# FNet mixing and an ELU layer: the first folds of x in another order, two column sums put off, and the middle token's second layer moved behind the last product

## The chip, the cores and the metric

One core of a Trainium2 chip runs the kernel. The metric is the device time in microseconds (us). Five engines work side by side, each through its own instructions in the order in which the program gives them: TensorE (PE in the profile, its weight loads PEld), VectorE (DVE), ScalarE (ACT), GpSimd (POOL) and SyncE (SP, which here issues DMAs). They wait for one another through semaphores.

## The reference

```python
X = np.fft.fft(x, axis=1)          # x: (8, 3008, 256)
X = np.fft.fft(X, axis=2)
x = X.real.reshape(8 * 3008, 256)
h = x @ w_in                       # w_in: (256, 2048)
g = np.where(h > 0.0, h, 1.0 * (np.exp(np.minimum(h, 0.0)) - 1.0))
return g @ w_out                   # w_out: (2048, 256)
```

All is float32 in value. The kernel receives the two weight matrices as 64-bit words and converts them itself.

## The kernel before

**The transform over the sequence** uses symmetry. A batch of x is loaded as four tiles `xl0` to `xl3` (in the code `L[0]` to `L[3]`), two by SP (first `L[3]`, then `L[0]`) and two by indirect DMAs of POOL (first `L[2]`, then `L[1]`). `fold_x` (L498) names its steps by keys. `e0` to `e3` add mirrored channels of a tile, `o0` to `o3` subtract them (one instruction of 128x768 each), `c0` to `c3` copy six columns that stand alone (128x6). `E0` adds e0 and e1, `E2` adds e2 and e3, `EO0` adds E0 and E2, `EO1` subtracts them; `O0`, `O2`, `EO2` and `EO3` do the same with the o tiles. For the first batch all of this is VectorE's work; `x1` (a row copied from `L[0]` to `L[1]`) and a one-element write that holds back `load_mats(1, 0)` are ScalarE's. `fold_first` (L549) makes four tiny sums of channel 128 of all four tiles.

A `Dft` (L607) is one product with a matrix of cosines or sines, in an even and an odd half (`mms`, six matmuls each on TensorE): `x_even` (channel 128, from `fold_first`), `R_even` (from EO0), `I_even` (from EO2), `R_odd` and `I_odd`. `copy` (ScalarE) and `unfold` (VectorE, two instructions) make the even half's columns. `plus` writes the lower 377 columns of the first 752 of a ring tile, `minus` the upper ones, one VectorE instruction each, both from the two halves (`R_even.minus` writes one column more). The rings are `Rr`, `Ir` and `Rb`; ScalarE copies Rb's rows 96 to 127 to `Ir` before `I_even` writes `Ir`.

**The two layers** run over tiles of 256 columns of the rings; a step is one tile with 256 of the 2048 hidden units. A step's first layer is `mm_P` (ring Rr, `bank("H")`), `even_part` (VectorE; reads Rb, `wex` and H, writes `E`), `mm_Q` (ring Ir), `h_minus`. Its ELU follows on ScalarE and VectorE, its second layer on TensorE. Two tiles are interleaved for the first 16 slots, so that slots 0 and 1 need the first chunk of `w_in`, slots 2 and 3 the second, and so on.

**The weights** come in 16 chunks. A chunk is converted by `fields` (two VectorE instructions, L256 and L262), `power` (for all but the first: three of ScalarE), `round` (GpSimd), `scale` (VectorE L310, then a GpSimd product, and for chunks of `w_in` two GpSimd sums, `pair`, written to `raw`). The first chunk is converted by VectorE alone except for one ScalarE instruction; its `scale` is L310 and L319. `fold_chunk(c)` (L427) multiplies a `w_in` chunk by the channel transform on TensorE; `put_chunk` (ScalarE) writes it to `Ws` and `Wc`. `turn_last_row` (TensorE) and `put_last_row` (ScalarE) make `wex`.

**Order.** Work is entered as events `at(t, fn)` (L1128); at the end they are sorted by t and run one after another. `pin` keeps each engine's instructions in that order. T is 4.8; negative times are the start. The events that are not part of the change and matter here: `dft_now(x_even)` at -13.1 and -13.08, `dft_now(R_even)` at -13.0 and -12.9, `turn_last_row(0)` at -10.6, `put_last_row(0)` at -10.59, `dft_now(I_even, 0)` at -10.5, `I_even.copy` at -1.8, `mm_P` of slot 0 at 0.0, `dft_now(I_even, 1)` at 0.05, `mm_P` of slot 1 at 0.1, `even_part` of slot 0 at 0.4, `I_even.unfold` at 0.5, `even_part` of slot 1 at 0.7, `fields` of the first `w_out` chunk at 0.96, EO1 at 1.3, `mm_Q` of slot 0 at 2.17, `fold_chunk(1)` at 2.3, `mm_Q` of slot 1 at 2.6, `dft_now(R_odd, 0)` at 3.1.

**The middle token** of every batch (position 1504) stands outside the rings. `mid_mm` (L1050) makes its hidden values for all eight batches, `mid_below`, `exp_neg` and `mid_g` its ELU, `mid_out` (L1067) its second layer (16 products, 32 matmul records), `mid_copy` takes the sums out, `mid_pick` (one product, two records) adds four row groups, `mid_store` takes them out and stores them by SP. There are 376 steps (`total`); `last` is 336.

**The end.** The last tile is combined and turned by VectorE in pieces (`comb_half`, `turn_half`); its stores are issued by SP and ACT in turn.

Of the kernel before, what the change touches and what calls it, by code (L numbers as in the profile page):

```python
# [18 lines left out]
ND = 256  # L19
# [3 lines left out]
RUN = HALF // 2  # L23
TW = 256
RING = 8 * TW
NE = 377
# [80 lines left out]
def kernel(  # L107
# [7 lines left out]
    nc = tc.nc  # L115
    NB = x.shape[0]
# [18 lines left out]
    pin = tc.keep_in_program_order  # L135
# [189 lines left out]
    def w1_dst(c):  # L325
        q, half = divmod(c, 2)
        if q not in w1:
            t = spool.tile([128, 1024], FP, tag="ot", bufs=2, name="w1")
            w1[q] = t.rearrange("p (h n) -> p h n", h=2)
        return w1[q][:, :, half * 256 : (half + 1) * 256]  # L330
# [17 lines left out]
    w1_chunks = [  # L348
        Chunk(
            moe_w_in[:, c * 256 : (c + 1) * 256].rearrange("(h p) n -> p h n", p=128),  # L350
            lambda c=c: w1_dst(c),
            IN_HOMES[c],
            IN_TMP[c],
            c > 0,
            c > 0,
        )
# [21 lines left out]
    def load_mats(ri, kodd, cuts=()):  # L378
        n = (2 * ri + kodd) * BW
        ends = (0, *cuts, BW)  # L380
        for a, z in zip(ends, ends[1:]):
            nc.sync.dma_start(
                out=MC[ri, kodd][:, a:z], in_=MC_dr.ap()[:, n + a : n + z]
            )
# [4 lines left out]
    Ir = cpool.tile([128, RING], FP, tag="Ir")  # L389
    Rb = cpool.tile([128, RING], FP, tag="Rb")  # L390
# [30 lines left out]
    def act(o, i, func=AF.Copy, **kw):  # L421
        pin(nc.scalar.activation(out=o, in_=i, func=func, **kw))  # L422
# [75 lines left out]
    def fold_x(L, engine_of, pieces):  # L498

        ops = {}  # L500

        def op(key, o, a, b, f):
            tt = lambda o, a, b, f: pin(
                engine_of(key).tensor_tensor(out=o, in0=a, in1=b, op=f)  # L504
            )
            n = o.shape[1]
            cuts = [n * i // pieces for i in range(pieces + 1)]
            for i in range(pieces):
                c = slice(cuts[i], cuts[i + 1])
                ops[key, i] = lambda c=c: tt(o[:, c], a[:, c], b[:, c], f)  # L510

        E, O = [], []
        for j in range(4):
            e = spool.tile([128, 6 * 128], FP, tag=f"e{j}", bufs=1, name=f"e{j}")
            o = spool.tile([128, 6 * 128], FP, tag=f"o{j}", bufs=1, name=f"o{j}")
            ev, ov = (
                t.rearrange("p (m o d) -> p m o d", o=2, d=64) for t in (e, o)
            )
            src = L[j].rearrange("p (m d) -> p m d", d=ND)
            if j in (1, 2):  # L520
                src = src[:, ::-1]

            lo, hi = (
                t.rearrange("p m (d o) -> p m o d", o=2)
                for t in (src[:, :, 1:129], src[:, :, 255:127:-1])
            )
            op(f"e{j}", ev, lo[:, :, ::-1], hi[:, :, ::-1], ALU.add)
            ops[f"c{j}", 0] = lambda e=ev[:, :, 0, 63:64], s=src[:, :, 0:1]: pin(
                engine_of("c").tensor_copy(out=e, in_=s)
            )  # L530
            op(f"o{j}", ov, lo, hi, ALU.subtract)
            E.append(e)
            O.append(o)
        ops["x1", 0] = lambda: act(L[1][0:1, 5 * ND :], L[0][0:1, 0:ND])
        op("E0", E[0], E[0], E[1], ALU.add)
        op("E2", E[2], E[2], E[3], ALU.add)
        op("EO0", E[1], E[0], E[2], ALU.add)
        op("EO1", E[3], E[0], E[2], ALU.subtract)
        op("O0", O[0], O[0], O[1], ALU.subtract)
        op("O2", O[2], O[2], O[3], ALU.subtract)  # L540
        op("EO2", O[1], O[0], O[2], ALU.subtract)
        op("EO3", O[3], O[0], O[2], ALU.add)
        return [E[1], E[3], O[1], O[3]], ops
# [5 lines left out]
    def fold_first(L):  # L549

        c = [t.rearrange("p (m d) -> p m d", d=ND)[:, :, 128:129] for t in L]
        c[1], c[2] = c[1][:, ::-1], c[2][:, ::-1]
        a = spool.tile([128, 6], FP, tag="xa", bufs=1, name="xa")
        g = spool.tile([128, 6], FP, tag="xg", bufs=1, name="xg")
        vtt(a.unsqueeze(2), c[0], c[1], ALU.add)
        vtt(g.unsqueeze(2), c[2], c[3], ALU.add)
        d = state["x_odd"] = spool.tile([128, 6], FP, tag="xd", bufs=1, name="xd")
        vtt(d, a, g, ALU.subtract)
        e = spool.tile([128, 6], FP, tag="xe0", bufs=1, name="xe0")
        vtt(e, a, g, ALU.add)  # L560
        return e
# [267 lines left out]
    def exp_neg(ap):  # L829
        act(ap, ap, func=AF.Exp, scale=-1.0)  # L830
# [247 lines left out]
            )  # L1078

    def mid_copy():  # L1080
        act(state["mh"][:, 0:ND], state["mo"][:, 0:ND])

    def mid_pick():
        po = state["mo"] = bank("H")
# [1 line left out]

    def mid_store():
        ob = state["mr"][0:NB, 0:ND]
        act(ob, state["mo"][0:NB, 0:ND])
        nc.sync.dma_start(  # L1090
            out=bass.AP(
                tensor=out.tensor,
                offset=out.offset + HALF * ND,
                ap=[[SEQ * ND, NB], [1, ND]],
            ),
            in_=ob,
        )

    state = {}
# [7 lines left out]
    for load in loads:  # L1107
        load()
    load_mats(0, 0, (BE,))
    w1_chunks[1].load()  # L1110
    nc.sync.dma_start(out=pick, in_=PK_dr.ap())
    EO, ops = fold_x(
        L_first, lambda key: nc.vector, 1
    )

    def fold_now(keys):
        for key in keys.split():
            ops[key, 0]()

    def dft_now(d, par, tag):  # L1120
        d.mms(par, bank(tag))

    R_even, I_even = Dft(0, 0, 0, EO[0]), Dft(1, 0, 0, EO[2])
# [4 lines left out]
    def at(t, fn):  # L1128
        events.append((t, len(events), fn))
# [16 lines left out]
    def begin_x_even():  # L1146
        state["x_even"] = Dft(0, 0, 0, fold_first(L_first), ring=Rb, first=True)

    at(-25.5, load_rest)
    at(-25.0, lambda: fold_now("e3 c3"))  # L1150
    at(-24.9, w1_chunks[0].scale)
    at(-24.8, lambda: fold_now("o3 e2 c2 E2 o2 O2"))
    at(-24.5, begin_x_even)
    at(-24.4, lambda: fold_now("e0 c0 e1 c1 E0 EO0"))
    at(-20.7, lambda: load_mats(1, 1))
    at(-20.6, w1_chunks[5].load)
    at(-20.5, w2_chunks[5].load)
# [4 lines left out]
    at(-13.08, lambda: dft_now(state["x_even"], 1, "pD"))  # L1162
    at(-13.0, lambda: dft_now(R_even, 0, "pA"))
    at(-12.9, lambda: dft_now(R_even, 1, "pB"))
    at(-11.1, lambda: state["x_even"].unfold())
    at(-11.0, lambda: fold_now("o0 o1 O0 EO2"))
    at(-10.95, R_even.copy)
    at(-10.94, R_even.unfold)
    at(-10.9, R_even.plus)
    at(-10.89, R_even.minus)  # L1170
    at(-10.85, lambda: state["x_even"].plus())
    at(-10.84, lambda: state["x_even"].minus())
    at(-10.83, lambda: act(Ir[96:128, 0:RUN], Rb[96:128, 0:RUN]))
    at(-10.92, w1_chunks[1].fields)
    at(-10.91, w1_chunks[1].power)
    at(-10.5, lambda: dft_now(I_even, 0, "pC"))
    at(-10.88, w1_chunks[1].round)
    at(0.05, lambda: dft_now(I_even, 1, "M"))
    at(-10.82, w1_chunks[1].scale)
    at(1.3, lambda: fold_now("EO1"))  # L1180

    T = PERIOD
    for chunk, k in (
# [22 lines left out]
        dt = first[k] if k < 4 else (-0.5, 0.05, 0.06, 2.95)  # L1206
# [24 lines left out]
    total = n_tiles * 8  # L1231
# [105 lines left out]
    def begin_folds(b):  # L1337
        state["EO"], state["ops"] = fold_x(state["L"], lambda key: nc.gpsimd, 2)

    steps_b = HALF * 8 // TW  # L1340
    for t, fn in (
        (-1.8, I_even.copy),
        (0.5, I_even.unfold),
        (0.6, I_even.plus),
        (0.8, I_even.minus),
        (3.1, lambda: dft_now(R_odd, 0, "pA")),
        (3.2, lambda: dft_now(R_odd, 1, "pB")),
        (T + 2.6, R_odd.copy),
        (T + 4.15, R_odd.unfold),
        (T + 4.2, R_odd.plus),  # L1350
        (T + 4.21, R_odd.minus),
    ):
        at(t, fn)
# [8 lines left out]
    for n in range(16):  # L1362
        j, k = divmod(n, 4)
# [17 lines left out]
    for b in range(1, NB):  # L1381
# [15 lines left out]
        n = 0  # L1397
# [16 lines left out]
    last = total - 40  # L1414
# [1 line left out]
        (last - 8) * T,  # L1416
        lambda: nc.sync.dma_start(out=Rx4[127:128, 0:NB], in_=r4_dr),
    )
    for n, (dt, fn) in enumerate(
        (  # L1420
            (4.75, mid_mm),
            (1.46, mid_below),
            (1.6, lambda: exp_neg(state["mr"])),
            (1.0, mid_g),
            (4.76, mid_out),
            (1.46, mid_copy),
            (4.75, mid_pick),
            (1.46, mid_store),
        )
    ):  # L1430
        at((last + n) * T + dt, fn)
    for _, _, fn in sorted(events, key=lambda e: e[:2]):
        fn()

# [29 lines left out]
```

## Time and profile before

| | |
|---|---|
| runs before (7) | median 1954.28 us, 1952.29 to 1955.21 |
| the profiled execution | 1954.53 us |
| its span, first to last instruction | 1952.5 us |
| busy: PE, PEld, DVE, ACT, POOL | 99%, 85%, 67%, 44%, 71% |
| granted TensorE clock, mean | 0.999 |

In the page's slices of the span (forty of 48.8 us each) PE is at nine tenths or more in all but the first and the last. A line of the timeline gives the start in us, the time taken, the engine, the line of the code (often a helper's, as L410 for all matmuls), the operation, the tile written and the tiles read, and in brackets how long the engine was idle just before and what ended that. A line of the table by stage gives, for each engine, the busy us and in brackets the number of instructions, then the granted clock of TensorE (PEclk), the busy share of the DMA engines and GB/s.

### The profile page before, as it was taken

The page shows a single profiled execution, that of the slowest core. Times are in us where ns is not written, and L with a number is a line of the kernel's source. Part 1 is how long each engine was busy: PE and PEld are TensorE (multiplying, and loading weights), DVE is VectorE, ACT ScalarE, POOL GpSimd, SP SyncE. Part 2 cuts the span into 40 slices and gives each one's busy share as a digit, 9 for nine tenths or more (in the row PEclk, how much of TensorE's full clock was granted, in tenths as well). Part 3 has the DMA queues.
Part 4 walks back from the last instruction along what each step waited for, and adds up shares of the span by engine and source line. Part 5 has one row for each costly group of instructions (what it writes and reads, how often), then busy time and mean ns, then how long its engine had stood idle before and what let it go on. Part 6 is the DMA issues. An engine that isn't in the chain of part 4 may idle for free.

```text
span 1952.5 us, 26991 instructions
## 1 busy us (share of the span) xinstructions
PE 1935.6 (99%) x8912; PEld 1652.9 (85%) x8912; DVE 1300.1 (67%) x2397; ACT 865.1 (44%) x1669; POOL 1379.3 (71%) x1816
## 2 busy tenths in 40 slices
PE   8999999999999999999999999999999999999998
PEld 5788788888888888888888888888888888888887
DVE  8976666666667666666666666676666666666666
ACT  3654444444444444444344444444434444444443
POOL 3888767776678766777677876777767776555655
PEclk9999999999999999999999999999999999999999
DMA  8246120101101021010210202012020110100101
GB/s 310 66 30 51 28 55 20 47 15 26 42 20 44 15 44 28 18 47 13 53 24 13 50 9 58 12 20 59 7 52 12 20 22 15 17 12 12 23 9 24
DMA packets 263290, 70.25 MB, mean 36 GB/s; under 512 B 248606, under 2 KB 249522, under 8 KB 263152
## 3 DMA queue, kind: packets, MB, share of 16 engines
q1 hardware_dynamic: 257360, 55.69, 15.0%
q0 software_dynamic: 3616, 12.59, 2.0%
q8 instruction: 70, 1.15, 0.2%
q14 instruction: 68, 0.56, 0.1%
q10 hardware_dynamic: 2176, 0.26, 0.1%
HBM read 43.66 MB, written 24.80 MB: 35 GB/s over the span
## 4 chain that ended last, share of the span: by engine, by line
PE 93%; DVE 3%; POOL 2%; issue 1%; ACT 1%; DMA 1%; SPq 0%; DVEq 0%; POOLq 0%
PE H L410 37%; PE pC L410 16%; PE pD L410 16%; PE pB L410 16%; PE pA L410 8%; POOL WT L419 1%; POOL w L419 1%; POOL G L419 0%; DMA xl<-in_x_dram 0%; DVE E L809 0%; DVE e L504 0%; DVE G L835 0%; DVE o L504 0%; DVE pow L310 0%; DMA xl<-in_x_dram,ix 0%
## 5 line engine op out<-in xcount | busy, mean ns | idle before, releaser
L419 POOL TENSOR_TENSOR G<-G 128x256 f32<-128x256 f32 x1440 | 1037.0, 730 | 511.2 <-DVE G L835 342.2
L809 DVE SCALAR_TENSOR_TENSOR E<-Rb,wex,H 128x256 f32<-128x256 f32 x752 | 327.8, 477 | 543.9 <-PE H L410 540.4
L422 ACT ACTIVATE G<-H 128x512 f32<-128x512 f32 x376 | 224.6, 597 | 959.0 <-DVE G L819 958.9
L410 PE MATMUL H<-Ir,Ws 128*128 128x256 f32 x1504 | 387.0, 380 | 3.7 <-DVE E L809 2.6
L410 PE MATMUL H<-Rr,Wc 128*128 128x256 f32 x1504 | 387.1, 380 | 0.1
L410 PE MATMUL pC<-G,WT 128*128 128x256 f32 x1440 | 369.5, 379 | 0.0
L410 PEld LDWEIGHTS H<-Rr,Wc 128*128 128x128 f32 x1504 | 284.5, 190 | 56.5 <-issue 3.4
L410 PEld LDWEIGHTS H<-Ir,Ws 128*128 128x128 f32 x1504 | 278.5, 189 | 52.0 <-DVE E L809 5.6
L410 PEld LDWEIGHTS pC<-G,WT 128*128 128x128 f32 x1440 | 273.6, 190 | 37.2
L819 DVE SCALAR_TENSOR_TENSOR G<-E,H 128x512 f32<-128x512 f32 x376 | 257.0, 684 | 41.7 <-POOL G L419 6.0
L835 DVE SCALAR_TENSOR_TENSOR G<-G,H 128x512 f32<-128x512 f32 x376 | 256.1, 681 | 42.7 <-ACT G L422 42.7
L835 DVE SCALAR_TENSOR_TENSOR G<-M,G 128x512 f32<-128x512 f32 x376 | 257.1, 684 | 0.0
L422 ACT ACTIVATE G<-G 128x512 f32<-128x512 f32 x376 | 233.2, 620 | 0.0
L410 PE MATMUL pD<-G,w 128*128 128x256 f32 x784 | 229.4, 379 | 0.5 <-POOL G L419 0.5
L410 PE MATMUL pA<-G,w 128*128 128x256 f32 x784 | 229.3, 379 | 0.6 <-DVE bs L416 0.6
L410 PE MATMUL pB<-G,w 128*128 128x256 f32 x784 | 229.3, 379 | 0.0
L422 ACT ACTIVATE M<-G 128x512 f32<-128x512 f32 x376 | 223.9, 596 | 0.0
L422 ACT ACTIVATE M<-M 128x512 f32<-128x512 f32 x376 | 221.0, 588 | 0.0
L410 PE MATMUL pB<-G,WT 128*128 128x256 f32 x720 | 214.8, 380 | 0.4
L410 PE MATMUL pD<-G,WT 128*128 128x256 f32 x720 | 214.1, 379 | 0.0
L410 PEld LDWEIGHTS pD<-G,w 128*128 128x128 f32 x784 | 148.9, 190 | 21.1 <-POOL G L419 0.9
L410 PEld LDWEIGHTS pA<-G,w 128*128 128x128 f32 x784 | 148.9, 190 | 21.1 <-issue 0.9
(145 smaller groups left out, 1416.7 us busy)
## 6 DMA issues: line engine op xcount, KB each, us to landing
out_dram<-ot SPq DMA_DIRECT2D x496, 32.0 KB
xl<-in_x_dram SPq DMA_DIRECT2D x16, 512.0 KB
xl<-in_x_dram SPq DMA_DIRECT2D x16, 256.0 KB
out_dram<-ot SPq DMA_DIRECT2D x256, 2.0 KB
Rb<-r SPq DMA_DIRECT2D x10, 376.0 KB
raw<-in_moe_w_in_dram SPq DMA_DIRECT2D x7, 512.0 KB
MC<-dft_mats SPq DMA_DIRECT2D x3, 943.5 KB
raw<-in_moe_w_out_dram SPq DMA_DIRECT2D x4, 512.0 KB
```

The lines of the kernel that those rows point to most:

```text
L410: nc.tensor.matmul(out_, lhsT=lhsT, rhs=rhs, start=start, stop=stop, skip_group_check=True)
L419: pin(nc.gpsimd.tensor_tensor(out=o, in0=a, in1=b, op=op))
L422: pin(nc.scalar.activation(out=o, in_=i, func=func, **kw))
L809: nc.vector.scalar_tensor_tensor(out=S.E[:, c], in0=Rb[:, cols(i)], scalar=wex[:, f : f + 1], in1=S.H[:, c], op0=ALU.mult, op1=ALU.add,)
L819: nc.vector.scalar_tensor_tensor(out=two(S.G[:, 0:512])[:, :, ::-1], in0=two(S.E), scalar=2.0, in1=two(S.H), op0=ALU.mult, op1=ALU.subtract,)
L835: nc.vector.scalar_tensor_tensor(out=o, in0=e, scalar=-1.0, in1=h, op0=ALU.add, op1=ALU.max)
```

## The change

- `c0`, `c2` and `c3` of the first batch go from VectorE to ScalarE; `c1` stays.
- `scale` of the first chunk moves ahead of `load_rest` and all folds.
- The folds on VectorE were e3 c3, [scale], o3 e2 c2 E2 o2 O2, [fold_first], e0 c0 e1 c1 E0 EO0, [x_even.unfold], o0 o1 O0 EO2. They become [scale], e3 c3 e0 c0 e2 c2 E2, [fold_first], e1 c1 E0 EO0, o3 o2 O2, [x_even.unfold], o0 o1 O0 EO2.
- After the unfolds, VectorE's order was fields of chunk 1, R_even.plus and minus, x_even.plus and minus, scale of chunk 1, even_part 0, I_even.unfold, I_even.plus, even_part 1, I_even.minus. It becomes R_even.plus, x_even.plus, fields of chunk 1, R_even.minus, even_part 0, I_even.unfold, I_even.plus, x_even.minus, I_even.minus, even_part 1, scale of chunk 1. ScalarE's copy of Rb to Ir is cut in two, one behind x_even.plus and ahead of `power` of chunk 1, one behind x_even.minus.
- `mid_out`, `mid_copy`, `mid_pick` and `mid_store` move from steps 340 to 343 behind the last product; `mid_copy` and `mid_store` read PSUM by VectorE in place of ScalarE, behind the last piece turned.

```diff
-            ops[f"c{j}", 0] = lambda e=ev[:, :, 0, 63:64], s=src[:, :, 0:1]: pin(
-                engine_of("c").tensor_copy(out=e, in_=s)
+            ops[f"c{j}", 0] = lambda e=ev[:, :, 0, 63:64], s=src[:, :, 0:1], j=j: (
+                act(e, s)
+                if engine_of("c") is nc.vector and j != 1
+                else pin(engine_of("c").tensor_copy(out=e, in_=s))
             )
...
     def mid_copy():
-        act(state["mh"][:, 0:ND], state["mo"][:, 0:ND])
+        pin(nc.vector.tensor_copy(out=state["mh"][:, 0:ND], in_=state["mo"][:, 0:ND]))
...
-        act(ob, state["mo"][0:NB, 0:ND])
+        pin(nc.vector.tensor_copy(out=ob, in_=state["mo"][0:NB, 0:ND]))
...
+    at(-25.6, w1_chunks[0].scale)
     at(-25.5, load_rest)
-    at(-25.0, lambda: fold_now("e3 c3"))
-    at(-24.9, w1_chunks[0].scale)
-    at(-24.8, lambda: fold_now("o3 e2 c2 E2 o2 O2"))
+    at(-25.0, lambda: fold_now("e3 c3 e0 c0 e2 c2 E2"))
     at(-24.5, begin_x_even)
-    at(-24.4, lambda: fold_now("e0 c0 e1 c1 E0 EO0"))
+    at(-24.4, lambda: fold_now("e1 c1 E0 EO0"))
...
-    at(-11.1, lambda: state["x_even"].unfold())
-    at(-11.0, lambda: fold_now("o0 o1 O0 EO2"))
+    at(-11.1, lambda: fold_now("o3 o2 O2"))
+    at(-11.0, lambda: state["x_even"].unfold())
+    at(-10.96, lambda: fold_now("o0 o1 O0 EO2"))
     at(-10.95, R_even.copy)
     at(-10.94, R_even.unfold)
     at(-10.9, R_even.plus)
-    at(-10.89, R_even.minus)
-    at(-10.85, lambda: state["x_even"].plus())
-    at(-10.84, lambda: state["x_even"].minus())
-    at(-10.83, lambda: act(Ir[96:128, 0:RUN], Rb[96:128, 0:RUN]))
-    at(-10.92, w1_chunks[1].fields)
-    at(-10.91, w1_chunks[1].power)
+    at(-10.89, lambda: state["x_even"].plus())
+    at(-10.885, lambda: act(Ir[96:128, 0:NE], Rb[96:128, 0:NE]))
+    at(-10.88, w1_chunks[1].fields)
+    at(-10.87, w1_chunks[1].power)
+    at(-10.86, w1_chunks[1].round)
+    at(-10.85, R_even.minus)
     at(-10.5, lambda: dft_now(I_even, 0, "pC"))
-    at(-10.88, w1_chunks[1].round)
     at(0.05, lambda: dft_now(I_even, 1, "M"))
-    at(-10.82, w1_chunks[1].scale)
+    at(0.6, lambda: state["x_even"].minus())
+    at(0.61, lambda: act(Ir[96:128, NE:RUN], Rb[96:128, NE:RUN]))
+    at(0.72, w1_chunks[1].scale)
...
-        (0.6, I_even.plus),
-        (0.8, I_even.minus),
+        (0.55, I_even.plus),
+        (0.65, I_even.minus),
...
-            (4.75, mid_mm),
-            (1.46, mid_below),
-            (1.6, lambda: exp_neg(state["mr"])),
-            (1.0, mid_g),
-            (4.76, mid_out),
-            (1.46, mid_copy),
-            (4.75, mid_pick),
-            (1.46, mid_store),
...
-        at((last + n) * T + dt, fn)
+    for n, dt, fn in (
+        (last, 4.75, mid_mm),
+        (last + 1, 1.46, mid_below),
+        (last + 2, 1.6, lambda: exp_neg(state["mr"])),
+        (last + 3, 1.0, mid_g),
+        (total + 1, 3.3, mid_out),
+        (total + 2, 2.9, mid_copy),
+        (total + 2, 2.91, mid_pick),
+        (total + 2, 2.92, mid_store),
+    ):
+        at(n * T + dt, fn)
```

More of the change, by code (lines that the diff above doesn't have):

```diff
@@ L1418 @@
     )
-    for n, (dt, fn) in enumerate(
-        (
-            (4.75, mid_mm),
-            (1.46, mid_below),
-            (1.6, lambda: exp_neg(state["mr"])),
-            (1.0, mid_g),
-            (4.76, mid_out),
-            (1.46, mid_copy),
-            (4.75, mid_pick),
-            (1.46, mid_store),
-        )
+    for n, dt, fn in (
[7 more added lines that the diff above has]
+        (total + 2, 2.92, mid_store),
     ):
-        at((last + n) * T + dt, fn)
+        at(n * T + dt, fn)
     for _, _, fn in sorted(events, key=lambda e: e[:2]):
```

## The prediction

> **What bounds the kernel now.** First the table by stage: where is TensorE full? (Columns as explained above; here the tail's clock is wanted too.)
>
> ```profile
> 14.00:34.00 20.00, 15.28 (x68) 9.97 (x68) 19.55 (x39) 4.54 (x11) 3.89 (x4) 1.00 1.04 400
> 34.00:60.00 26.00, 24.78 (x116) 18.61 (x114) 24.97 (x43) 18.72 (x38) 16.46 (x15) 1.00 0.45 160
> 60.00:1946.00 1886.00, 1882.64 (x8684) 1619.25 (x8684) 1247.88 (x2298) 839.25 (x1616) 1354.07 (x1787) 1.00 0.15 28
> 1946.10:1948.90 2.80, 0.00 (x0) 0.00 (x0) 2.43 (x7) 0.00 (x0) 0.00 (x0) 1.00 0.60 91
> 1948.90:1952.40 3.50, 0.00 (x0) 0.00 (x0) 0.00 (x0) 0.00 (x0) 0.00 (x0) 0.50 0.51 78
> ```
>
> From 60 us to the last product TensorE is busy 1882.6 of 1886 us, from 34 to 60 us 24.8 of 26. So a delay of TensorE at 34 us reaches the end nearly whole, and a product taken out of the middle is worth its time on TensorE. Before 34 us VectorE sets the pace (19.55 of 20). Next the timeline of the head:
>
> ```profile
> 10.47 0.96 DVE L504 TENSOR_TENSOR e<-xl 128x768 f32<-128x768 f32 x1 [4.42 <-DMA xl<-in_x_dram]
> ...
> 13.47 0.42 ACT L422 ACTIVATE xl<-xl 1x256 f32<-1x256 f32 x1 [7.73 <-DMA xl<-in_x_dram,ix]
> ...
> 29.34 1.30 POOL L419 TENSOR_TENSOR w<-raw,w 128x512 f32<-128x512 f32 x1 [22.46 <-DMA Wc<-in_moe_w_in_dram]
> 29.56 1.63 DVE L310 SCALAR_TENSOR_TENSOR pow<-raw,pow 128x512 int32<-128x512 int32 x1
> ...
> 31.11 0.86 DVE L809 SCALAR_TENSOR_TENSOR E<-Rb,wex,H 128x256 f32<-128x256 f32 x2
> ...
> 31.33 1.27 POOL L419 TENSOR_TENSOR w<-w,pow 128x512 f32<-128x512 f32 x1 [0.69 <-DVE pow L310]
> ...
> 32.60 0.55 DVE L416 TENSOR_TENSOR Ir<-bs,M 127x377 f32<-127x377 f32 x1
> 32.68 1.42 POOL L419 TENSOR_TENSOR raw<-w 128x256 f32<-128x256 f32 x2
> ...
> 33.29 1.10 PE L410 MATMUL H<-Ir,Ws 128*128 128x256 f32 x4 [1.13 <-DVE Ir L416]
> ...
> 34.32 1.08 PE L410 MATMUL H<-raw,CC 128*64 128x256 f32 x8
> ```
>
> See the chain of chunk 1 of w_in: L310 (its scale) at 29.56, the GpSimd product at 31.33, the two sums at 32.68, ending 34.10, and fold_chunk(1) on TensorE at 34.32, just when mm_Q of slot 0 (33.29) is done. It has no slack, and mm_Q of slot 1 and all later products stand behind it.
>
> **The first folds.** By the trace's landing events the last pieces came at 10.37 (L3), 11.41 (L2), 14.07 (L0) and 14.56 (L1); the ACT row above, which waits for L1's larger load until 13.47, fits them. A fold that needs no result of the one ahead starts 0.88 after it; one that does, 1.0. The new order puts e0 second: it starts at 14.17, so VectorE idles 14.17 - 11.35 = 2.82 us, where before it had scale and o3, e2. Taken from that stretch: scale of chunk 0 (11.54 to 12.87, 1.33; it fits into the idle time before 10.47), c3 and c0 (1.07 less 0.88, 0.19 each). c2 now goes VectorE, ScalarE, VectorE: +0.10, taken from the 0.17 to 0.20 us of small ACT rows and two hand-overs. Sum up to EO2: +2.82 - 1.33 - 0.38 + 0.10 = **+1.21 us**.
> Inside this stretch the parts come in another order. fold_first ends 0.47 earlier (e0 14.17, e2 15.05, E2 16.32, sums 17.20), so x_even's products start at 17.8 (18.24). EO0 would be ready at 20.8, but TensorE is in x_even's odd half until 21.2: R_even starts at 21.2 (22.37), 1.2 us earlier. It waits then: EO2, and with it I_even's first half, comes at 27.87 (26.66). c3, c0 and c2 on ScalarE stand behind x1 and the one-element write, which wait for L1 until 14.58 and end at 14.78, ahead of e0's end at 15.13: nothing but E2's 0.10. scale passes load_rest, but not a wait: its DMAs are SP's and keep their order.
>
> **The lower columns first.** R_even.unfold 26.48 + 1.21 = 27.69; plus follows a dependent 0.70 later (as 40.77 to 41.47) at 28.39, ends 28.94. But mm_P of slot 0 stands behind I_even's first half (27.87 + 1.39): it starts at 29.26 (28.27). I_even's second half ends at 32.3.
> x_even.plus 28.85, fields 29.30 and 29.64, R_even.minus 29.98. ScalarE: the half copy at 29.46 (0.83 for 752 columns, so about 0.5), power 29.96 to 31.76 (its three took 27.45 to 29.25), then wex; even_part 0 needs wex: 31.95 (31.11). I_even.unfold 32.75, plus 33.45 to 34.0, mm_Q of slot 0 34.1 (33.29): **+0.8**, ending 35.2.
>
> **Chunk 1 late.** x_even.minus 33.9 to 34.45; the second half copy on ScalarE to 35.0; I_even.minus must wait for it, as both write Ir: 35.1; even_part 1 35.55; only then L310 of chunk 1, 36.35 to 37.0. GpSimd: product (1.3) and two sums (0.7 each) with hand-overs: 37.1 to 39.9. fold_chunk(1) at 40.0 at the earliest. VectorE has the next chunk's fields and EO1 behind L310, between SBUF tiles only, and such rows alternate with GpSimd's (L310 at 29.56 took 1.63 in place of 0.68 beside the product at 29.34): 0.3 and 0.9 us go in between, which gives 41.1. Before, 34.32: **+5.7 to +6.8**; I take 6.8. TensorE idles from 35.2 to 41.1, 5.9 us (4.8 at the least).
> Later waits in the old trace shrink: 0.57 at 41.51 (R_odd.unfold) and 0.56 at 44.03 (even_part of slot 2). Worked through, VectorE and ScalarE trail TensorE there by about the same amount, but these two waits go: -1.0. The waits after 44 us (0.56 at 60.46, 0.48 at 108.8) end chains that start behind the same step; I leave them. Head: **+5.8** (4.7 to 5.8; if all of the later waits went too, 1.0 less).
>
> **The clock.** In the table above the granted clock fell to 0.50 at 1948.9, 2.8 us after the last product (1946.1). Gaps of up to 2.3 us (before 18.24) left it at 1.00. The new gap is twice the one that sufficed. At the start, the weight loads of the warm-up products came 0.43 us apart until 6.67 and 0.21 after (32 in 6.87), 5.5 us after the first product. So TensorE would run at half speed for up to 5.5 us behind the gap and lose half of that, 2.8. Bounds: 0 (no fall) to 2.8. I take **+1.9**, two thirds of the upper end: a fall is likely, but part of the slow stretch can lie in the gap itself.
> The Trainium skill ("TensorE: Matmul & The Clock Gate", section "What's actually happening") speaks against the change here: the clock halves after an idle window of some 3.4 us, and windows run freely. By that rule alone an estimate would be a fall in (5.9 - 3.4) / 3.4, three of four runs, and nothing in the fourth; the tail's row, with 2.8 us, says every run.
>
> **The middle token.** Two rows carry what goes:
>
> ```profile
> 1770.68 1.93 PE L410 MATMUL H<-w,mid 128*32 128x256 f32 x32
> ...
> 1782.24 0.62 PE L410 MATMUL H<-mid,pick 128*32 128x256 f32 x2
> ...
> 1948.22 0.45 DVE L992 STREAM_TRANSPOSE ot<-v 128x256 f32<-128x256 f32 x1
> ```
>
> A step lasts 4.75 us (mm_P 1925.34 to 1930.09). From the end of mm_P at 1766.87 to that at 1773.68 it took 6.81, from 1778.43 to 1783.92 5.49: mid_out costs 2.06, mid_pick 0.74, **-2.8**. Behind the last product mid_out (1946.1 to about 1948.2) lies beside VectorE's last sums and turns. What is late next is the new chain behind the last turn: mid_copy 1948.6 (0.4), mid_pick (0.6 to 0.9), mid_store (0.4, by the 128x256 row 0.38), SP's issue, ready at about 1950.25. SP's issues ended at 1949.95 before, so the last store leaves some 0.5 to 1 us later: **+0.7** (0.4 to 1.3). The two copies leave ScalarE, which waits for VectorE there (2.6 us a step): nothing.
>
> **Sum.** 1954.53 (the profiled execution, 2.0 around its span of 1952.5) + 5.8 + 1.9 - 2.8 + 0.7 = 1960.1. That execution lies 0.25 above the median: **1960.0**.
>
> **The rivals.**
> *The clock holds* in the gap: 1960.0 - 1.9 = 1958.1. For it: the fall at 1948.9 came after TensorE's last work, not in a gap. Against: nothing tells TensorE that its work is over.
> *It falls earlier too.* R_even ends at 24.6 and I_even starts at 27.87; only four one-column products lie between. If that gap (3.3 us) halves the clock, I_even's halves and two mm_P (6 us) take some 2.5 longer: 1962.5.
> *Not slower: fold_chunk(1) finds its data.* If L310 of chunk 1 can run before even_part 0, the stall is gone: TensorE goes on at +0.8, 1954.3 + 0.8 - 2.1 = 1953.0. It decides from L310 at about 32.1 (35.2 less 3.1 for the GpSimd part). Against: VectorE's rows stand in the order of the events throughout the old trace.
> *All as the words say*: L0 lands with L2 and the 2.8 us of idling go, so that the head gains about 2 and chunk 1 is not late: 1954.3 - 2.0 - 2.1 = 1950.2. Against: the landings above, and two conditions at once.
>
> **How the numbers follow.** Forecast 0.52 (1958.5 to 1961); clock holds 0.18; earlier fall 0.12; not slower 0.12; all as the words say 0.06. A measurement of this kernel tells 0.2% (3.9 us: 1950.4 and 1958.2) from no change. Faster: 0.06. Same: 0.12 and half of the second case (it stands on the bound), 0.21. Slower: 0.73. The range leaves out the last two cases. Low end: head 4.7, clock 0, middle token -2.4: 1954.3 + 2.3 = 1956.5. High end: 5.8 + 2.8 + 2.5 - 1.5 = 9.6: 1964.0.
>
> **What would show it.** e on VectorE idle for 2.8 us up to 14.17; R_even's products at 21.2; mm_Q of slot 0 at 34.1; L310 of chunk 1 behind the second E at 36 to 37; fold_chunk(1) at 40 to 41 with TensorE idle for 5 to 6 us, and its clock at half in the next few; mm_P of slot 2 at 47 to 49 (39.92); steps from 60 us on shifted by 6 to 8 us; 2.8 less between 1765 and 1785; the store of mid last. Wrong I would be if VectorE's order differs from that of the events, if L0 lands earlier, or if the chains between 46 and 60 us have slack that I did not see.

## The result and the profile after

| | before | after |
|---|---|---|
| median of the runs, us | 1953.81 (35 runs, 1952.23 to 1956.23) | 1958.48 (15 runs, 1957.7 to 1961.37) |
| the profiled execution, its span, us | 1954.53, 1952.5 | 1959.0, 1957.2 |
| granted TensorE clock, mean | 0.999 | 0.997 |

The ratio after to before is 1.0025 (95%: 1.0019 to 1.0032): slower, by little more than the 0.2% that can be told from no change. First the table by stage of the changed kernel, in the stretches of the old one (PE, PEld, DVE, ACT, POOL busy, then the granted clock):

```profile
14.00:34.00 20.00, 15.34 (x58) 10.49 (x55) 16.38 (x33) 4.50 (x14) 1.29 (x1) 0.83 1.03 399
34.00:60.00 26.00, 20.23 (x86) 14.51 (x85) 21.53 (x35) 14.22 (x30) 13.86 (x11) 0.87 0.35 123
60.00:1946.00 1886.00, 1883.23 (x8668) 1620.89 (x8667) 1253.36 (x2308) 843.05 (x1624) 1354.71 (x1788) 1.00 0.16 29
```

All is lost before 60 us: between 34 and 60 us TensorE is busy 20.23 us in place of 24.78, and its mean clock is 0.87 there and 0.83 in the 20 us ahead, in place of 1.00. From 60 us on TensorE is as full as before. The timeline of the changed kernel's head, in which the steps of the prediction can be looked up:

```profile
13.12 1.83 DVE L504 TENSOR_TENSOR e<-xl 128x768 f32<-128x768 f32 x2 [3.43 <-DMA xl<-in_x_dram]
...
26.76 2.86 PE L410 MATMUL pC<-MC,o 128*128 128x189 f32 x6 [3.11 <-issue]
...
31.44 0.87 DVE L811 SCALAR_TENSOR_TENSOR E<-Rb,wex,H 128x256 f32<-128x256 f32 x2 [1.95 <-ACT anti L422]
...
34.57 1.10 PE L410 MATMUL H<-Ir,Ws 128*128 128x256 f32 x4
...
35.92 0.86 DVE L811 SCALAR_TENSOR_TENSOR E<-Rb,wex,H 128x256 f32<-128x256 f32 x2
36.70 0.68 DVE L310 SCALAR_TENSOR_TENSOR pow<-raw,pow 128x512 int32<-128x512 int32 x1
...
37.52 1.32 POOL L419 TENSOR_TENSOR w<-w,pow 128x512 f32<-128x512 f32 x1 [5.48 <-DVE pow L310]
37.64 1.50 DVE L262 TENSOR_SCALAR w<-w 128x512 int32<-128x512 int32 x1
...
38.93 2.19 POOL L419 TENSOR_TENSOR raw<-w 128x256 f32<-128x256 f32 x2
39.05 1.48 DVE L504 TENSOR_TENSOR e<-e,e 128x768 f32<-128x768 f32 x1
...
41.17 1.97 PE L410 MATMUL H<-raw,CC 128*64 128x256 f32 x8 [5.50 <-POOL raw L419]
...
49.12 1.02 PE L410 MATMUL H<-Rr,Wc 128*128 128x256 f32 x4
```

See three things. VectorE stands idle for 3.43 us until `xl0` lands and e0 can start (13.12). (TensorE's idle 3.11 us ahead of I_even at 26.76 are put down to "issue"; EO2, which I_even reads, ended on VectorE at 26.66.) L310 of chunk 1 stands behind the second E, at 36.70, where before it ran at 29.56; GpSimd had waited 5.48 us for it. And fold_chunk(1) starts at 41.17, TensorE having stood idle for 5.50 us, and takes 1.97 us for what took 1.08. At the other end, the timeline behind the last product:

```profile
1950.65 1.93 PE L410 MATMUL H<-w,mid 128*32 128x256 f32 x32
...
1952.90 0.45 DVE L994 STREAM_TRANSPOSE ot<-v 128x256 f32<-128x256 f32 x1
...
1953.71 0.62 PE L410 MATMUL H<-mid,pick 128*32 128x256 f32 x2 [1.13 <-DVE mid L1083]
...
1954.81 0.29 SPq L1092 DMA_DIRECT2D out_dram<-mid  x1
```

`mid_out` lies beside VectorE's last sums and turns; its store is the last.

**The account.** With the starts of five kinds of products as marks, the difference of the two spans (4.7 us) falls into seven pieces, each beside what the prediction gave it:

| from, to | before | after | difference | predicted |
|---|---|---|---|---|
| start to I_even's first half | 26.66 | 26.76 | +0.10 | +1.21 |
| to mm_Q of slot 0 | 6.63 | 7.81 | +1.18 | -0.40 |
| to fold_chunk(1) | 1.03 | 6.60 | +5.57 | +5.97 |
| to mm_P of slot 2 | 5.60 | 7.95 | +2.35 | +1.9 |
| to fold_chunk(2) | 6.90 | 5.80 | -1.10 | -1.0 |
| to the end of the last product | 1899.21 | 1895.79 | -3.42 | -2.8 |
| to the end of the span | 6.47 | 6.49 | +0.02 | +0.7 |
| sum | 1952.5 | 1957.2 | +4.70 | +5.6 |

### The profile page after: what moved, and what is told of

Its sections match the earlier page's. It is cut to its first block, busy times and chain, and to the rows that moved or that the text cites. A ratio compares the mean times of both kernels' runs of the same rounds, so it can differ in the third digit from the quotient of the medians.

```text
span 1957.2 us, 26996 instructions
## 1 busy us (share of the span) xinstructions
PE 1938.9 (99%) x8912; PEld 1656.0 (85%) x8912; DVE 1301.7 (67%) x2396; ACT 864.8 (44%) x1671; POOL 1377.3 (70%) x1816
## 4 chain that ended last, share of the span: by engine, by line
PE 95%; DVE 2%; POOL 1%; issue 1%; DMA 1%; ACT 0%; SPq 0%; DVEq 0%; POOLq 0%
PE H L410 38%; PE pB L410 16%; PE pC L410 16%; PE pD L410 16%; PE pA L410 8%; POOL WT L419 1%; DMA xl<-in_x_dram 1%; POOL w L419 0%; DVE E L811 0%; POOL G L419 0%; DVE G L837 0%; DVE pow L310 0%; DVE v L416 0%; DVE G L821 0%; PE M L410 0%
```

## The experiments

The theory is that of the prediction: chunk 1's L310, put behind even_part 1, starves TensorE, the gap halves its clock on top, and the middle token gives some 2.8 us back. The rivals put the loss elsewhere: into the folds' order alone, or into the clock alone. Every kernel is compared with the kernel before on the same chip; the ratios are to that. Names as `landing_order` are those that the expectations use.

**1. The middle token alone** (`mid_only`). The kernel before with the last hunk of the diff (the events of `mid_*`) and the two copies by VectorE.

> The kernel before with the move of the middle token's second layer alone. Theory (the change loses in the head, by a stall of TensorE in front of fold_chunk(1) and by its clock): no gap in the head; mid_out and mid_pick leave the full stretch, -2.8 us, and the last store lands 0.1 us later behind the last product (5.47 us after it in the changed kernel, 5.36 before): 2.7 us faster than before, 1951.1. Rival (the new tail costs what the middle gains): 1953.8, no change.

Measured: 1951.09 us (11 runs) against 1953.01, ratio 0.9988 (0.9979 to 0.9997). The stretch from fold_chunk(2) to the end of the last product is 1896.33 us, 2.88 shorter than before, and what lies behind the last product 6.54 (6.47 before). So this part is a gain of its own, and what it puts behind the last product costs next to nothing.

A second run of the same kernel, on another chip and beside kernel 9 below:

> mid_only once more, beside the version with both the folds and the middle token changed. Theory: 2.0 to 2.7 faster than before; slower than landing_awake by 0.5 to 1. Rival (the folds' order gives nothing): level with landing_awake.

Measured: 1950.49 (11 runs) against 1952.92, ratio 0.9986 (0.9977 to 0.9995); the same stretch took 1896.35. The gain is below the 0.2% named above, but both intervals lie under 1 and both profiles show where it comes from.

**2. The head alone.** The kernel after with `mid_out` to `mid_store` at steps 340 to 343 and their copies on ScalarE, as before.

> The changed kernel with the middle token where it was before. Theory: all of the loss is in the head, 7.5 us (last product 4.7 us later in the changed kernel, plus the 2.8 that the middle gives): 1961.3. Rival (part of the loss is in the tail): 1957 to 1959.

Measured: 1962.19 (5 runs) against 1953.01, ratio 1.0044 (1.0031 to 1.0058). The head alone loses some 8.6 us by the ratio, where 7.5 was expected. Its spans differ by 7.9 (1960.4 and 1952.5), in the pieces of the account: +1.55, -0.44, +5.58, +2.45, -1.09, -0.16 and 0.01.

**3. Chunk 1's scale where it was.** One event of the kernel after (F1 in the expectation is fold_chunk(1)):

```diff
-    at(0.72, w1_chunks[1].scale)
+    at(-10.82, w1_chunks[1].scale)
```

> The changed kernel with one line back: scale of chunk 1 ahead of even_part 0, as before. Theory: L310 of chunk 1 at about 31, the GpSimd sums end near 36, TensorE stalls 1 us in place of 5.5 in front of fold_chunk(1) and its clock does not fall there; F1 1.8 us later than before in place of 6.8, the middle token -2.7: 1952.5 to 1954.5 (the upper end if the clock still falls in the gap ahead of I_even). Rival (the loss is VectorE's idle time in front of e0, 2.8 us, and what follows from it): 1957 or more.

Measured: 1953.55 (11 runs) against 1953.01, ratio 1.0000 (0.9991 to 1.0009). TensorE in the timeline:

```profile
36.10 1.10 PE L410 MATMUL H<-Ir,Ws 128*128 128x256 f32 x4
37.13 1.08 PE L410 MATMUL H<-raw,CC 128*64 128x256 f32 x8
```

fold_chunk(1) stands right behind mm_Q of slot 0: the stall is gone, by this event alone. That mm_Q is late itself (36.10): the clock fell at 27.34 in this execution and stayed down for 6.83 us, and I_even's first half to mm_Q took 8.02.

The rest of the head still loses something. This kernel has the middle token's gain, and yet each of its runs was slower than each run of kernel 1 on the same chip (1952.27 and more against 1952.25 and less), by 2.5 us in the medians. In the two profiles I_even starts 1.0 later than in kernel 1, behind VectorE's wait for `xl0` (2.78 us), and the stretches from there to fold_chunk(2) take 2.5 us longer in sum, with the clock down for part of them.

**4. The same event moved in the kernel before**, as the only edit (the reverse of the diff above).

> The kernel before with one line of the change: scale of chunk 1 behind even_part 1 (0.72 in place of -10.82). Theory: L310 of chunk 1 moves from 29.6 to about 33.8, the GpSimd sums end 3.4 us later, fold_chunk(1) starts at 37.8 in place of 34.3; 0.5 us of that goes in later waits: 2.8 us slower than before (1955.8), up to 4.5 slower if the clock falls in the gap of 3.5 us. Rival (the place of scale alone costs nothing, the folds' new order does): 1953.0.

Measured: 1957.95 (9 runs) against 1953.13, ratio 1.0025 (1.0015 to 1.0034): 4.8 us slower, a little more than the 2.8 to 4.5 that were expected. Its timeline, from an execution that was the shortest of its nine (1955.53):

```profile
31.14 1.10 PE L410 MATMUL H<-Ir,Ws 128*128 128x256 f32 x4 [0.77 <-DVE Ir L416]
35.58 1.84 PE L410 MATMUL H<-raw,CC 128*64 128x256 f32 x8 [3.33 <-POOL raw L419]
```

The stall and the slow clock behind it (1.84 in place of 1.08) come with this one event, in a kernel whose folds, sums and middle token are the old ones. Its ratio is that of the whole change. So the event is needed for the loss (3), and alone it is enough for a loss of that size (4). It is not the whole of the head's 8.6 us (2): by the ratios of 3 and 4 it is worth some 4.8 or 4.9. In the changed order the stall is longer, too: from mm_Q to fold_chunk(1) it is 6.60 us there and 4.44 here. There x_even.minus, ScalarE's second copy and I_even.minus come in between I_even.plus and even_part 1, and so ahead of L310; here they don't. The wait for `xl0` is another part (3).

**5. The clock held up.** Products of zeros, whose sums the next real product overwrites, fill TensorE's two gaps in the kernel after (they are work added to the kernel):

```diff
+    def keep_awake(ps, n):
+        for _ in range(n):
+            mm(ps, zero, zero[:, 0:1].to_broadcast([128, 512]), True)
...
         ps = folds[c] = bank("H")
+        if c == 1:
+            keep_awake(ps, 24)
...
     def dft_now(d, par, tag):
-        d.mms(par, bank(tag))
+        ps = bank(tag)
+        if d is I_even and not par:
+            keep_awake(ps, 10)
+        d.mms(par, ps)
```

> The changed kernel with idle products of zeros (128x512, bf16, as in the warm-up) in the two gaps of TensorE: 10 ahead of I_even's first half, 24 ahead of fold_chunk(1), into banks that the next product starts anew. Theory: the granted clock stays at 1.00, fold_chunk(1) still starts at about 41 with the sums of GpSimd, but the products behind it run at full speed (2.4 us less between 41.2 and 46.1), and I_even.plus comes up to 0.9 earlier: 1955.2 to 1956.2. Rival (the clock is not the bound there, VectorE and GpSimd are): 1958.5.

Measured: 1956.7 (11 runs) against 1953.01, ratio 1.0017 (1.0008 to 1.0026), 0.5 us above what was expected. From its timeline:

```profile
27.09 1.54 PE L410 MATMUL pC<-MC,o 128*128 128x189 f32 x6 [0.87 <-DVE o L510]
...
34.27 5.39 PE L410 MATMUL H<-zero 128*128 128x512 bf16 x24
39.94 1.08 PE L410 MATMUL H<-raw,CC 128*64 128x256 f32 x8 [0.28 <-POOL raw L419]
...
45.53 1.02 PE L410 MATMUL H<-Rr,Wc 128*128 128x256 f32 x4
...
69.13 1.13 PE L410 MATMUL H<-Ir,Ws 128*128 128x256 f32 x4 [1.07 <-DVE E L817]
```

The granted clock is 1.00 throughout. The stall is as long as before (mm_Q to fold_chunk(1) 6.61 us, 6.60 in the kernel after), so it is the data's and not the clock's. I_even's first half to mm_Q takes 6.24 in place of 7.81, fold_chunk(1) to mm_P of slot 2 takes 5.59 in place of 7.95: the clock's two falls cost 1.57 and 2.36 us. Of these 3.9 us, the profiled span shows 2.3 (1954.9 against 1957.2): I_even began 0.33 later, and 1.07 came back at 69.13 as a wait for E that the kernel after doesn't have there. The intervals of the two ratios overlap; the share of the clock is shown by the profiles, not by the times.

**6. Only the first gap filled** (the 10 products ahead of I_even).

> The changed kernel with 10 idle products of zeros in the first gap alone, ahead of I_even's first half. Theory: the first fall of the clock does not come, I_even.plus and mm_Q of slot 0 are up to 0.9 earlier, fold_chunk(1) by the same; the second fall stays: 0.5 to 0.9 faster than the changed kernel, 1957 to 1957.7. Rival (the first fall is hidden behind VectorE and ScalarE): 1958.3, as the changed kernel.

Measured: 1958.99 (7 runs) against 1953.13, ratio 1.0028 (1.0017 to 1.0039): no gain, which was not expected. The first fall was gone (I_even to mm_Q 6.24), but the second, behind the gap that was left, came at 36.73 instead of 39.25 and lasted 10.24 us instead of 6.83: fold_chunk(1) to mm_P of slot 2 took 8.56 in place of 7.95. The rest of this execution's 1958.3 us can't be set beside the 1957.2 of the kernel after: e0 started 1.28 later (14.40), and the stretch behind the last product took 7.15 in place of 6.49.

**7. The folds in the order of landing, without idling** (`landing_order`). The kernel after with o3 and E2 ahead of e0, and all copies c back on VectorE:

```diff
-    at(-25.0, lambda: fold_now("e3 c3 e0 c0 e2 c2 E2"))
+    at(-25.0, lambda: fold_now("e3 c3 e2 c2 E2 o3 e0 c0"))
...
-    at(-11.1, lambda: fold_now("o3 o2 O2"))
+    at(-11.1, lambda: fold_now("o2 O2"))
```

> The changed kernel with the folds in the order in which the loads land (e3 c3 e2 c2 E2 o3, then e0 c0), all c on VectorE, scale of chunk 1 late as changed. Theory: VectorE no longer idles in front of e0, the head up to mm_Q of slot 0 comes 2.5 us earlier, but fold_chunk(1) still stalls TensorE for 6 us (scale comes earlier by the same 2.5): 2.5 faster than the changed kernel, 1955.5, and still 2 slower than before. Rival (the idle time in front of e0 is the loss, 4.5 us and more with what follows): 1951 or less.

Measured: 1956.53 (12 runs, one of them far off at 2257.59, which the ratio leaves out) against 1953.13, ratio 1.0015 (1.0007 to 1.0024), 1.0 above what was expected. I_even's first half started at 25.87; the stall is unchanged (mm_Q to fold_chunk(1) 6.60), and so is the fall of the clock (to mm_P of slot 2 7.94).

**8. That order and the early scale** (7 and 3 together, `landing_early`).

> As landing_order, and scale of chunk 1 early as before; the middle token as changed. Theory: mm_Q of slot 0 1.8 us earlier than before, fold_chunk(1) 0.8 earlier, 0.6 left at mm_Q of slot 2, the middle token 2.7: 3.3 faster than before, 1949.7, if the clock holds in the first gap (2.4 us). Rival (only one of the two edits counts): 1951 to 1952.

Measured: 1950.88 (11 runs) against 1953.13, ratio 0.9987 (0.9978 to 0.9996), 1.2 us above what was expected. Hardly a stall (0.39 us, fold_chunk(1) at 34.02), but the clock fell at 27.09 for 3.41 us.

**9. The same with 8 products of zeros ahead of I_even** (`landing_awake`).

> As landing_early, with 8 idle products of zeros ahead of I_even's first half. Theory (in landing_early the clock fell at 27.09 for 3.4 us, behind a gap of 2.2 us, and took back what the folds' order gained): the clock holds, I_even's second half ends 0.9 earlier, mm_Q of slot 0 up to 0.9 earlier; GpSimd's sums then bind fold_chunk(1), so 0.3 to 0.9 faster than landing_early: 1950.0 to 1950.6. Rival (VectorE and GpSimd bind anyway): 1950.9.

Measured: 1951.24 (11 runs) against 1952.92, ratio 0.9991 (0.9982 to 1.0000). A miss: the clock fell in another place. The table by stage of this kernel:

```profile
30.31:33.72 3.41, 1.45 (x7) 0.86 (x8) 2.73 (x8) 0.51 (x1) 3.02 (x4) 1.00 1.01 392
33.72:37.14 3.42, 3.42 (x12) 2.01 (x11) 2.78 (x6) 2.95 (x7) 1.13 (x1) 0.50 0.82 228
```

TensorE, set going earlier, then waited 1.08 us for I_even.plus and 0.89 for chunk 1 and was busy 1.45 of 3.41 us; in the next stretch the clock is 0.50. And 8 and 9 are no faster than the middle token alone (0.9988 and 0.9986): the order of landing gave nothing over the old order that can be measured, and the order of the change lost something (3). The best versions measured are those of 1 and 8, 0.12 to 0.14% below the kernel before, and 1 is the smaller edit.

## Why the prediction was right, and where its terms were not

The sum came out (predicted 1960.0, +5.6; measured 1958.48, +4.7), and its main mechanism is shown by kernels 3 and 4. (Its last line is rounded: 1960.1 less 0.25 is 1959.9.) By its steps:

- **The first folds**, +1.21. In the account it is +0.10, but `xl0` happened to land 1.04 us earlier in that execution (13.03 against 14.07), so +1.14 for the same landings; in the head alone, where e0 started at 14.56 instead of the 14.17 of the prediction, it is +1.55, less 0.39: +1.16. The term was right.
- **The lower columns first**, 27.87 to 34.1: 6.23 predicted, 6.19 in the head alone and 6.24 with the clock held up. Right at full clock; in the kernel after it took 7.81.
- **Chunk 1 late**, 7.0 from mm_Q to fold_chunk(1): 6.60, 6.61 and 6.61 in three kernels. Right, 0.4 too long. The alternation of VectorE's SBUF rows with GpSimd's, counted as 0.3 and 0.9, is seen: the two sums took 2.19 us in place of 1.42, L262 beside the product 1.50 (0.42 alone).
- **The clock**, +1.9, forecast as one fall. The fall behind fold_chunk(1) cost 2.36 (within the bounds). There was a second, in the gap ahead of I_even, from 25.59: the rival *it falls earlier too* happened along with the forecast, and its price was 1.57, not 2.5. It used up the 1.04 us that the early landing gave. In the head alone, which has the same head but other landings, the early slow stretch lay ahead of that gap, at about 18.8 to 22.2, where R_even's start was late (23.09) but I_even waited for VectorE anyway. So this other fall moves from execution to execution, with what it costs. The prediction went by the length of a gap; what decided is told in the last section.
- **Later waits**, -1.0: -1.10. The wait of 0.56 us at 60.46, which the prediction left standing, is gone too; this was a term missed. Of the -3.42 behind fold_chunk(2), 2.88 is the middle token, and the other 0.54 fits that wait; kernel 4, without the middle token's move, shows 0.53 (1898.68), but the head alone, in which the wait is gone as well, only 0.16. Where the rest went in that execution's 1899 us isn't known.
- **The middle token**, -2.8: -2.88 and -2.86 in the two runs of it alone. Right.
- **The tail**, +0.7: +0.02 (0.07 and 0.09 in the two runs of the middle token alone). This was the term that was mis-sized outside its bounds (0.4 to 1.3). The last issue ended 0.37 later behind the last product than before (4.39 against 4.02), as the chain of copies and mid_pick made it, but it landed 1.08 us after, where the last store of before needed 1.34. That store is 8 rows of 1 KB, the other is made of pieces of 128 bytes.

By the account the change is 4.70 where 5.58 was predicted: the landing (1.1), the tail (0.7), the waits behind mm_P of slot 2 (0.7) and the stall (0.4) took off 2.9, the clock's two falls put 2.0 on. That the errors nearly cancelled was luck: the forecast was closer than its terms. The rival *the clock holds* is out by the profile, *not slower* and *all as the words say* by L310 at 36.70 and by e0's wait.

Left open: whether an order of the folds can gain anything over the old one. The landings of x move by 1 us and more between executions of one kernel (the first fold started at 10.88 and at 9.44 us in the two profiles of kernel 1), and the clock's falls move with them. Only 8 or 10 zero products in the first gap and 24 in the second were tried, no pattern fitted to the falls.

## What to carry to other kernels

Before a conversion is moved behind other work of an engine, follow its chain to the product that needs it: here one instruction of 0.68 us, put 7 us later, with three GpSimd operations behind it, held up every later product. Work that must be done at some time (the middle token's second layer) cost next to nothing beside a tail in which its engine is idle anyway. And a gap on the engine that sets the pace can cost more than its length: ahead of fold_chunk(1), 5.5 us of waiting brought a slow clock that cost 2.4 us more.

## What the runs showed of the clock that was not expected

The granted clock changes on a grid of 3.413 us that starts elsewhere in each execution. In the kernel after the changes stand at 25.59, 32.42, 39.25 and 46.07, two steps apart each time; in one where the head has none, the grid is counted on from the rise in the warm-up. The kernel after, in windows of its grid:

```profile
22.18:25.59 3.41, 1.47 (x8) 0.98 (x6) 3.38 (x6) 0.00 (x0) 0.00 (x0) 1.00 1.00 393
25.59:29.01 3.42, 2.25 (x6) 1.99 (x7) 3.28 (x9) 0.66 (x2) 0.00 (x0) 0.50 1.07 396
29.01:32.42 3.41, 3.41 (x8) 2.17 (x8) 1.46 (x5) 1.92 (x5) 1.29 (x1) 0.50 1.00 397
32.42:35.83 3.41, 3.25 (x13) 1.99 (x11) 1.79 (x5) 0.51 (x1) 0.00 (x0) 1.00 1.06 394
35.83:39.25 3.42, 0.00 (x0) 0.00 (x0) 3.42 (x7) 1.36 (x3) 1.65 (x2) 1.00 0.46 179
39.25:42.66 3.41, 1.49 (x8) 0.76 (x8) 3.01 (x3) 0.55 (x1) 3.41 (x3) 0.50 0.00 0
42.66:46.07 3.41, 3.41 (x12) 2.64 (x9) 0.89 (x2) 2.67 (x6) 1.43 (x2) 0.50 0.45 124
```

A window at 1.00 in which PE was busy 1.47 of 3.41 us is followed by one at 0.50; so is one with 0.00. A window at 0.50 in which PE was busy all the time is followed by one at 1.00; one with 2.25 is not. The same reading of all 12 profiled executions, from the warm-up to 56 us:

| window at | TensorE busy share | the next window |
|---|---|---|
| full clock | 0 to 0.43 (12 windows) | half, every time |
| full clock | 0.46 and more | full, every time |
| half clock | 0 to 0.80 (7 windows) | half, every time |
| half clock | 1.00 (12 windows) | full, every time |

The border is seen only to lie between 0.43 (the first row above) and 0.46, the middle token alone:

```profile
16.81:20.22 3.41, 1.57 (x7) 1.31 (x8) 3.31 (x9) 0.00 (x0) 0.00 (x0) 1.00 1.07 406
```

So slow stretches lasted 3.41, 6.83 or 10.24 us, by how soon a fully busy window came, and a gap of 2.2 us (ahead of I_even in kernel 8) was enough where little else lay in its window. The Trainium skill ("TensorE: Matmul & The Clock Gate", section "What's actually happening") has the same free-running window of 3413 ns, but asks for an idle one; here a window need not be idle, and the measurement decides. Kernels 6 and 9 fit this. In kernel 9 the gap ahead of I_even was filled, another window (1.45 of 3.41) held too little work, and the fall came behind that one. In kernel 6 the longer gap was left, and its grid lay so that two windows at half clock, the last two lines here, were not full:

```profile
33.32:36.73 3.41, 1.10 (x4) 0.68 (x4) 2.73 (x7) 0.51 (x1) 0.01 (x1) 1.00 1.05 395
36.73:40.14 3.41, 0.00 (x0) 0.00 (x0) 3.41 (x5) 1.91 (x3) 2.87 (x3) 0.50 0.24 91
40.14:43.56 3.42, 2.73 (x10) 1.51 (x11) 1.78 (x3) 0.70 (x3) 3.34 (x3) 0.50 0.00 0
```
